# A chunked linear recurrence and a mixture of experts: decays and y kept in the buffer that w is loaded into, and a new order of steps

## The chip, the cores and the metric

The kernel runs on one core of one Trainium2 chip. The metric is the device time of one execution in microseconds (us). The engines are TensorE (PE for its matmuls, PEld for its weight loads), VectorE (DVE), ScalarE (ACT), GpSimd (POOL) and SyncE (SP, which here only issues transfers). Each engine takes its instructions strictly in the order in which the program gives them to it, and waits on semaphores where an instruction needs another engine's result.

## The reference

Two parts follow one another. The first is a recurrence over 768 steps, for 4 batches of 8 heads, each with a 40 x 40 state:

```python
for t in range(S):                       # r, k, v, w, a, b: (4, 8, 768, 40)
    y[:, :, t] = einsum('bhd,bhde->bhe', r_t, state)
    Sa = einsum('bhde,bhe->bhd', state, a_t)
    state = state * w_t[:, :, None, :] - einsum('bhd,bhe->bhde', Sa, b_t)
    state = state + einsum('bhd,bhe->bhde', v_t, k_t)
```

The second takes y as 3072 rows of 320 and sends each row to one of 8 experts: logits = x @ w_gate, the largest logit names the expert and its softmax is the weight, at most 768 rows go to an expert, in order of the rows; each expert computes relu(x @ w1) @ w2 with a hidden width of 1024, and the weight scales its row of the output.

## The kernel before

**Tiling.** The 768 steps are cut into six blocks i of 128, and a block into two chunks c of 64. The four batches make two pairs, pr = 0 and 1; a pair's two batches lie on partitions 0 to 39 and 64 to 103 of a buffer, each half of 64 partitions, so instructions that span both work on 104 partitions and rows 40 to 63 must hold zeros (or values that meet zeros).

**Stages of one block.** `prep` loads `w`, `a`, `kb` and `rv` and makes the decays on DVE: `scan_g` (L315) a scan from right to left into `gx`, `scan_p` (L325) one from left to right into `px`; `mul_a` (L331) and `mul_kb` (L336) multiply them into `a` and `kb`. `unit` makes three products per chunk: `nn`, which ACT copies into `ns`; `kk`, which DVE masks into `tm` (L381); and `iden`, which ACT copies into `bk`. `inverse` inverts the triangular matrices of both pairs and both chunks together on DVE: a transpose `begin2` (L485), 31 pairs of rows (L432 a product into `tmp`, L433 a sum into `nu`), called the elimination here, and two transposes back, `back_a` (L437) and `back_b` (L441); `comb` (L453, L469) puts the 32-wide parts together on PE and ACT to `nt`. `chain` then walks the chunks: from the state (`D` for pair 0, `E` for pair 1) over `zs`, `vu` and `snew` to the next state (DVE L596, L599), and aside from that `qp` (a mask on DVE, L640) and y. `take_y` (L667) scales y by `px` into `yE`. `gate` transposes y (L711), makes the logits (L716), and stores the rows; `route` places them with indirect transfers. When all six blocks are routed, a count of the fullest expert is cast to an integer (`maxc`, L1229), on whose value a branch hangs, and the experts follow with weights streamed from memory.

**What sets the order.** The code of a stage doesn't run where it is written: `steps(name)` collects threads of steps, each with the engine it uses and a planner's time for it, what it needs and gives, and which buffers it takes and frees. `Schedule.order` plays these threads against each other with those times and emits the steps in the order that results; a table `later` can move a thread, and `mu` and `tail` weigh the due time and the length of what follows. A step can't be placed before its buffers are free. `BUFS` says how many there are of each: three of `px`, two each of `w` and `yE`. A `px` is taken in `scan_p` and freed by the second chunk's `take_y`:

```python
add(scan_p, "V2.8", take=["px"], free=["w"], gives=("px", n))
...
more(take_y, "V.69", take=["yE"] * (1 - c), free=["pp"] + ["px"] * c, gives=("y", n))
```

**Start.** DVE clears PSUM, `w` and a helper `z2`; POOL clears rows 32 to 63 and 96 to 127 of `a`, `kb` and `rv` (L262), then other buffers, `gx`'s last column (L266) among the later ones.

## Time and profile before

| | |
|---|---|
| median of 3 runs (lowest to highest) | 921.32 us (919.52 to 922.74) |
| the profiled execution: time, and its span | 922.49 us, 920.8 us |
| busy: PE, DVE, ACT, POOL | 611.3, 463.2, 212.5, 155.7 us |
| mean granted TensorE clock, as a share of the full one | 0.782 |
| recurrence with routing; experts | to 639; from 639 to 921 us |

The span runs from the first to the last instruction of the profiled execution. An engine's busy time is a sum over stages that have different limits. The TensorE clock has two levels, 1.2 GHz (0.50) and 2.4 GHz (1.00); a value between them is a mean over a stretch.

### The profile page before, as it was taken

The numbers are of one execution on the slowest core, as the hardware profiler recorded it, in microseconds if no ns is written. First come the engines' busy times: TensorE is split into PE (matmuls) and PEld (weight loads), VectorE is DVE, ScalarE is ACT, GpSimd is POOL, SyncE is SP. The second block draws the span as 40 slices with busy tenths as digits, with TensorE's granted clock in tenths as the row PEclk, the third lists the DMA queues.
The fourth block names the chain that finished last, engine by engine and source line by source line (L and its number), as shares of the span: only waits on it lengthen the run. The fifth ranks groups of instructions, "written<-read, shape, count | busy, mean of one in ns | idle before, by whom it ended". The sixth has DMA issues, their size and how long they took to land. (4 is left out here: it accounts for less than half of the span.)

```text
span 920.8 us, 30344 instructions
## 1 busy us (share of the span) xinstructions
PE 611.3 (66%) x13828; PEld 483.9 (53%) x13828; DVE 463.2 (50%) x853; ACT 212.5 (23%) x444; POOL 155.7 (17%) x203
## 2 busy tenths in 40 slices
PE   0306776197836877198736886385079999988893
PEld 0305666196736766197636776385026665445542
DVE  5794339923686256923587347733423334432320
ACT  0002322022112222032111222121324333442230
POOL 9700000001000010001000100011333233223321
PEclk9957997569655897558765797577579999999987
DMA  3401133022401143012320212001985855576410
GB/s 97 140 22 48 40 88 83 1 73 69 89 15 57 40 74 103 1 38 75 53 84 1 49 37 59 18 4 47 243 133 145 198 129 148 155 203 154 126 50 17
DMA packets 77662, 73.83 MB, mean 80 GB/s; under 512 B 46857, under 2 KB 69387, under 8 KB 75604
## 3 DMA queue, kind: packets, MB, share of 16 engines
q1 hardware_dynamic: 68116, 54.50, 24.3%
q0 software_dynamic: 4224, 9.89, 3.7%
q10 hardware_dynamic: 5184, 7.41, 2.9%
q8 instruction: 110, 1.80, 0.9%
q14 instruction: 28, 0.23, 0.1%
HBM read 56.77 MB, written 10.08 MB: 73 GB/s over the span
## 5 line engine op out<-in xcount | busy, mean ns | idle before, releaser
L1142 PE MATMUL ps<-xT,w 128*128 128x480 f16 (+1 forms) x512 | 112.7, 387 | 49.2 <-DMA mm<-meta 36.4
L977 DVE SCALAR_TENSOR_TENSOR w<-s,w 128x640 f16<-128x640 f32 (+1 forms) x56 | 54.0, 994 | 110.0 <-ACT w L976 109.7
L1142 PEld LDWEIGHTS <-w 128*128 128x128 f16 (+1 forms) x512 | 46.6, 101 | 114.8 <-issue 78.3
L1037 PE MATMUL ps<-w,hh 128*128 128x320 f16 (+1 forms) x768 | 106.1, 299 | 0.0
L1037 PEld LDWEIGHTS <-hh 128*128 128x128 f16 (+1 forms) x768 | 79.0, 104 | 26.4 <-issue 1.1
L252 PE MATMUL p<-a,kb 64*64 64x64 f32 x768 | 43.2, 294 | 62.6 <-DVE a L331 58.1
L976 ACT ACTIVATE w<-s 128x640 f16<-128x640 f32 (+1 forms) x56 | 46.6, 871 | 116.6 <-DMA s<-in_moe_w_dram 111.9
L453 PE MATMUL p<-nu,ns 32*32 32x32 f32 x768 | 22.3, 233 | 77.1 <-DVE nu L441 42.0
L252 PEld LDWEIGHTS p<-a,kb 64*64 64x64 f32 x768 | 39.3, 202 | 64.4 <-DVE a L331 58.4
L433 DVE TENSOR_TENSOR nu<-nu,tmp 128x31 f32<-128x31 f32 (+15 forms) x186 | 63.8, 343 | 6.4
L432 DVE TENSOR_TENSOR tmp<-xu,nu 128x31 f32<-128x31 f32 (+15 forms) x186 | 63.6, 342 | 6.5
L1152 DVE SCALAR_TENSOR_TENSOR hh<-ps,hh 128x480 f16<-128x480 f32 x64 | 39.0, 651 | 53.1 <-ACT hh L1149 53.0
L453 PEld LDWEIGHTS p<-nu,ns 32*32 32x32 f32 x768 | 20.7, 148 | 78.4 <-DVE nu L441 42.5
L424 POOL MEMSET nu<- 128x1024 f32 x6 | 5.7, 953 | 328.1 <-PE p L453 328.1
L1041 POOL DMA_INDIRECT out_dram<-ob,ri x32 | 34.8, 1088 | 149.9 <-ACT ob L1168 76.1
L252 PE MATMUL pp<-a,kb 64*32 64x64 f32 (+1 forms) x1536 | 32.0, 257 | 39.9 <-DVE z L314 36.8
L902 POOL DMA_INDIRECT meta<-mt,sloti x24 | 23.7, 986 | 186.6 <-DVE mt L899 146.3
L252 PEld LDWEIGHTS pp<-a,kb 64*32 64x32 f32 x1536 | 28.7, 138 | 42.8 <-issue 34.9
L640 DVE TENSOR_TENSOR qp<-pp,mask 128x1024 f32<-128x1024 f32 x24 | 29.1, 1221 | 27.0 <-PE pp L252 26.8
L252 PE MATMUL pp<-ident,kb 64*64 64x40 f32 x1536 | 33.6, 241 | 12.8 <-issue 9.3
L381 DVE TENSOR_TENSOR tm<-p,mask 128x512 f32<-128x512 f32 x24 | 16.3, 681 | 51.3 <-PE p L252 51.1
L1149 ACT ACTIVATE hh<-ps 128x480 f16<-128x480 f32 x64 | 32.9, 566 | 35.2 <-PE ps L1142 35.1
(141 smaller groups left out, 1024.3 us busy)
## 6 DMA issues: line engine op xcount, KB each, us to landing
s<-in_moe_w_dram SPq DMA_DIRECT2D x16, 512.0 KB
kb<-in_kb_dram SPq DMA_DIRECT2D x24, 320.0 KB
rv<-in_rv_dram SPq DMA_DIRECT2D x24, 320.0 KB
s<-in_moe_w_dram ACTq DMA_DIRECT2D x17, 320.0 KB
...
```

The lines of the kernel that those rows point to most:

```text
L252: TT.matmul(out, l, r, start=start, stop=True, skip_group_check=True)
L432: V.tensor_mul(tv, xu[:, s + 1:, s:s + 1].to_broadcast([P, n, m]), nu[:, s:s + 1, 0:m].to_broadcast([P, n, m]))
L433: V.tensor_add(nu[:, s + 1:, 0:m], nu[:, s + 1:, 0:m], tv)
L453: TT.matmul(p[C * z + 32:C * z + 64, u * 32:u * 32 + 32], G_["ns"][lo, pr * 16 + u, 32:C], s_["n1"][lo, pr * 16 + u, :], start=True, stop= ...
L640: V.tensor_mul(U["qp"].rearrange("p r u t -> p (r u) t"), U["pm"].rearrange("p r (u t) -> p (r u) t", t=C), mk(16))
L976: return (lambda: nc.scalar.activation(h, s(), AF.Copy, scale=SW), lambda: nc.vector.scalar_tensor_tensor(l, s(), SW, h, ALU.mult, ALU.sub ...
L977: lambda: nc.vector.scalar_tensor_tensor(l, s(), SW, h, ALU.mult, ALU.subtract))
L1037: nc.tensor.matmul(po[:, :DM], h[l], rr[:, f, :], start=(f == 0 and m == 0), stop=(f == NF - 1 and m == 2))
L1041: nc.gpsimd.indirect_dma_start(out=out[:, :], out_offset=bass.IndirectOffsetOnAxis(ap=ri.bitcast(U32)[:c, j, 1:2], axis=0), in_=ob[:c], in ...
L1142: nc.tensor.matmul(s_["h", f + z][:, :n], l, rr, start=m % 7 == 0 and m < 14, stop=m >= 14)
L1149: nc.scalar.activation(s_["hh"][:, 0, f, :n], s_["h", f][:, :n], AF.Relu)
L1152: nc.vector.scalar_tensor_tensor(s_["hh"][:, 1, f, :n], s_["h", f][:, :n], 0.0, s_["hh"][:, 0, f, :n], ALU.max, ALU.subtract)
```

## The change

`w` is loaded into `px` itself, one column to the right, by one transfer of 128 partitions (the host packs a third group of rows so that all 128 are defined) in place of two of 40; column 0 is cleared by DVE in `scan_g`. `scan_p` and `take_y` write where they read, so that `px` holds w, then the decay, then the scaled y, and is freed after the logits; `w` and `yE` go. There are six `px`, and one more of `a`, `tm` and `nt`. Zero rows of `a`, `kb` and `rv` come by 16 transfers from a cleared tile of 24 rows. The logits are made in quarters: for each head, each half of the partitions (a batch) and each half of the columns (a chunk) a matmul of its own. The planner's times for some steps, its latencies and weights are other numbers, and `later` has a table; of those numbers a few lines stand here. A choice between ACT and DVE for a copy goes to DVE only where it would end 1.05 us earlier by the planner.

```diff
@@ -156,7 +156,7 @@
                         ends.append(z + d[-1] + 0.9)
                         end = max(end, ends[-1])
                     else:
-                        end = max(end, s0 + hold + 0.12)
+                        end = max(end, s0 + hold + (0.34 if e == "P" else 0.14))
...
-    MU = 0.004
-    O_TAIL = 0.004
+    MU = 0.0036902
+    O_TAIL = 0.0016952
...
-    BUFS = {"pp": 3, "p1": 2, "w": 2, "gx": 1, "px": 3, "a": 3, "kb": 2, "rv": 2, "tm": 4, "ns": 1, "xu": 1, "nu": 1,
-            "nt": 3, "qq": 1, "bk": 5, "vu": 4, "zs": 2, "uE": 2, "qp": 2, "Sd": 3, "yE": 2, "x16": 2, "D": 2, "E": 2,
+    BUFS = {"pp": 3, "p1": 2, "gx": 1, "px": 6, "a": 4, "kb": 2, "rv": 2, "tm": 5, "ns": 1, "xu": 1, "nu": 1,
+            "nt": 4, "qq": 1, "bk": 5, "vu": 4, "zs": 2, "uE": 2, "qp": 2, "Sd": 3, "x16": 2, "D": 2, "E": 2,
             "g0": 4}
...
-    sch = Schedule(nc, free_, MU, O_TAIL, O_BIAS, (0.8, 0.0, 0.0), {})
+    LATER = {"chain": -0.01, "comb": -0.66, "decay": 0.12, "decay_k": 0.2, "fill": 36.07, "gate": -0.24,
+             "iden": -0.05, "inverse": 0.1, "inverse_": -46.42, "kk": -0.36, "load_a": 1.12, "load_kb": -1.45,
+             "load_rv": 7.56, "load_v": 5.54, "load_w": -2.65, "lower": 0.24, "nn": -1.22, "out": -0.04,
+             "route": 0.03, "saT": -18.52, "turn": 0.48, "unit": -16.96, "zz": 0.22}
+    sch = Schedule(nc, free_, MU, O_TAIL, O_BIAS, (1.05,) * 3, LATER)
...
-    for n, x in enumerate(free_["pp"] + free_["p1"]):
+    zero = one.tile([24, 2 * H * P], F32, name="zero")
+    V.memset(zero, 0.0)
+    z2 = one.tile([P, H, P + 1], F32, name="z2")
+    V.memset(z2, 0.0)
+    for x in free_["a"] + free_["kb"] + free_["rv"]:
+        n = x.rearrange(("p h t -> p (h t)", "p z h t -> p (z h t)", "p z c u t -> p (z c u t)")[len(x.shape) - 3])
+        for lo in (D, C + D):
+            nc.sync.dma_start(n[lo:lo + 24], zero[:, 0:n.shape[1]])
+    for x in free_["pp"] + free_["p1"]:
         V.memset(x, 0.0)
-    for n, x in enumerate(free_["w"]):
-        (V, G)[n % 2].memset(x, 1.0)
-        (V, G)[n % 2].memset(x[:, :, 0:1], 0.0)
-    for n, x in enumerate(free_["a"] + free_["kb"] + free_["rv"]):
-        for lo in (32, 96):
-            G.memset(x[lo:lo + 32], 0.0)
     for x in free_["zs"] + free_["D"] + free_["E"]:
```

```diff
+        def load_w():
+            T["px"] = get("px")
+            dma(T["px"][:, :, 1:], w[pr, i].rearrange("e (h t) -> e h t", h=H))
+
+        steps("load_w")(load_w, "L0>2.7", take=["px"], gives=("load_w", n))
...
             if i:
                 T["g0"] = get("g0")
             V.memset(z2[0:R, :, 0:1], 1.0)
+            V.memset(T["px"][:, :, 0:1], 0.0)
             V.tensor_tensor_scan(T["gx"][0:R, 0:H * (P + 1)][:, ::-1],
-                                 T["w"][0:R].rearrange("p h t -> p (h t)")[:, ::-1],
+                                 T["px"][0:R].rearrange("p h t -> p (h t)")[:, ::-1],
                                  z2[0:R].rearrange("p h t -> p (h t)")[:, ::-1], 1.0, ALU.mult, ALU.add)
 
         def scan_p():
-            T["px"] = get("px")
             g3 = T["gx"][0:R, 0:H * (P + 1)].rearrange("p (h t) -> p h t", t=P + 1)
             if i:
                 V.tensor_copy(T["g0"][0:R, :], g3[:, :, 1])
             V.reciprocal(z2[0:R, :, 0], g3[:, :, 1])
             V.tensor_tensor_scan(T["px"][0:R].rearrange("p h t -> p (h t)"),
-                                 T["w"][0:R].rearrange("p h t -> p (h t)"),
+                                 T["px"][0:R].rearrange("p h t -> p (h t)"),
                                  z2[0:R].rearrange("p h t -> p (h t)"), 1.0, ALU.mult, ALU.add)
-            put("w", T["w"])
...
         add = steps(f"decay{pr}")
-        add(scan_g, "V2.5", take=["gx"] + ["g0"] * (i > 0), needs=[("load_w", n)])
-        add(scan_p, "V2.8", take=["px"], free=["w"], gives=("px", n))
+        add(scan_g, "V2.7", take=["gx"] + ["g0"] * (i > 0), needs=[("load_w", n)])
+        add(scan_p, "V2.8", gives=("px", n))
...
         def take_y():
-            if c == 0:
-                T["yE"] = get("yE")
             p = U["py"]
-            V.scalar_tensor_tensor(T["yE"][0:R, :, ct].rearrange("p (r k) t -> p r k t", r=2),
+            V.scalar_tensor_tensor(T["px"][0:R, :, ct].rearrange("p (r k) t -> p r k t", r=2),
                                    p[0:R, :, 0:256].rearrange("p r (k t) -> p r k t", k=4), SX,
                                    T["px"][0:R, :, ct].rearrange("p (r k) t -> p r k t", r=2), ALU.mult, ALU.mult)
             put("pp", p)
-            if c:
-                put("px", T["px"])
...
@@ -695,9 +697,9 @@
         more(mT_v, "P.65", needs=[("load_rv", (pr, i)), ("uE", n)], take=["pp"])
         more(mT_u, "P.65", needs=[("uE", n)], free=["uE"])
         more(take_m, "V1.22", take=["qp"], free=["pp"])
-        more(yy, "P1.6", needs=[("bk", n)] + [("Sd", n)] * (q > 0), take=["pp"],
+        more(yy, "P1.6", needs=[("bk", n)] + [("Sd", n)] * (q > 0) + [("snew", n)] * (q < NQ - 1), take=["pp"],
              free=["qp", "bk", "vu"] + ["Sd"] * (q > 0) + ["rv"] * c)
-        more(take_y, "V.69", take=["yE"] * (1 - c), free=["pp"] + ["px"] * c, gives=("y", n))
+        more(take_y, "V.69", free=["pp"], gives=("y", n))
...
     def gate(T):
@@ -708,13 +710,15 @@
         def turn_y():
             p = Q["pt"] = get("pp")
             for h in range(H):
-                TT.transpose(p[:, h // 4, h % 4 * P:h % 4 * P + R], T["yE"][0:R, h, :], ident[0:R, 0:R])
+                TT.transpose(p[:, h // 4, h % 4 * P:h % 4 * P + R], T["px"][0:R, h, 0:P], ident[0:R, 0:R])
 
         def logits():
             p = Q["pt"]
             for h in range(H):
-                TT.matmul(p[:, 0, R:R + 16], T["yE"][0:R, h, :], wge[0:R, h, :], start=h == 0, stop=h == H - 1)
-            put("yE", T["yE"])
+                for x in range(2):
+                    for c in range(2):
+                        mm(p[half(c), x, R:R + 8], T["px"][half(x), h, half(c)], wge[half(x), h, :], h == 0)
+            put("px", T["px"])
...
         def take_logits():
             t = pr * NI + i
-            scale(lg[:, t::2 * NI, :], Q["pt"][:, 0, R:R + 16].rearrange("p (x e) -> p x e", x=2), 1.0 / SX)
...
-    wge = glob.tile([104, H, 2 * E], F32, name="wge")
+    wge = glob.tile([P, H, E], F32, name="wge")
     nc.gpsimd.memset(wge, 0.0)
     for x in range(2):
-        nc.sync.dma_start(wge[64 * x:64 * x + D, :, x * E:x * E + E], w_gate.rearrange("(h d) e -> d h e", d=D))
+        nc.sync.dma_start(wge[64 * x:64 * x + D], w_gate.rearrange("(h d) e -> d h e", d=D))
...
     out = {x: inputs[x] for x in ("moe_w_gate", "moe_w1", "moe_w2", "moe_capacity")}
-    out["w"] = rows(inputs["w"])
+    x = rows(inputs["w"])
+    out["w"] = np.concatenate([x, x[:, :, :, 0:C - D]], 3).reshape(B // 2, NI, P, H * P)
```

How the order moves, in three places. Rows are an engine's instructions in their order: source line, operation, what is written <- what is read, with buffer numbers, and the shape. First DVE, ahead of and into the elimination of block 2 (the third), before; L667 is the last y of block 1, pair 1, L325 the second decay of block 2, L485 `begin2`:

```order
L596 TENSOR_TENSOR E_153<-p_1_103,g_3_157 104x8x40
L667 SCALAR_TENSOR_TENSOR yE_147<-pp_101,px_107 104x8x64
L323 COPY g_0_154<-gx_106 104x8
L324 RECIPROCAL z_188<-gx_106 104x8
L325 SCALAR_TENSOR_TENSOR px_107<-w_104,z_188 104x1032
L336 TENSOR_TENSOR kb_113<-kb_113,gx_106 104x2048
L485 STREAM_TRANSPOSE xu_122<-ns_121 128x1024
L432 TENSOR_TENSOR tmp<-xu_122,nu_123 128x31
L433 TENSOR_TENSOR nu_123<-nu_123,tmp 128x31
```

and in the changed kernel, eleven rows in the elimination of block 2, from its seventh row on (L438 and L439 are the former L432 and L433, L605 the new state of block 1, L387 a masked `tm`, L646 a `qp`):

```order
L438 TENSOR_TENSOR tmp<-xu_125,nu_126 128x112
L439 TENSOR_TENSOR nu_126<-nu_126,tmp 128x28x4
L605 TENSOR_TENSOR D_152<-p_0_102,D_153 104x8x40
L438 TENSOR_TENSOR tmp<-xu_125,nu_126 128x135
L439 TENSOR_TENSOR nu_126<-nu_126,tmp 128x27x5
L387 TENSOR_TENSOR tm_120<-p_1_103,mask 128x512
L646 TENSOR_TENSOR qp_145<-pp_99,mask 128x1024
L438 TENSOR_TENSOR tmp<-xu_125,nu_126 128x156
L439 TENSOR_TENSOR nu_126<-nu_126,tmp 128x26x6
L438 TENSOR_TENSOR tmp<-xu_125,nu_126 128x175
L439 TENSOR_TENSOR nu_126<-nu_126,tmp 128x25x7
```

The elimination stood in one piece behind the last y of the block before; now its pairs of rows stand between the steps of the chain of block 1, from the first new state on (in blocks 1 to 5 alike, 62 rows in groups of 2 to 10).

Second SP's queue, the first transfers before:

```order
L828 DMA wge<-in_moe_w_gate_dram 40x8x8 x2
L62 DMA w_104<-in_w_dram 40x8x128 x2
L62 DMA kb_113<-in_kb_dram 40x2048 x2
L62 DMA a_110<-in_a_dram 40x1024 x2
L62 DMA w_105<-in_w_dram 40x8x128 x2
L62 DMA vu_133<-in_vt_dram 64x320 x2
L62 DMA rv_115<-in_rv_dram 40x2048 x2
```

and now (`zero` is the cleared tile, a_111 to rv_118 the buffers that get zero rows):

```order
L62 DMA px_105<-in_w_dram 128x8x128
L832 DMA wge<-in_moe_w_gate_dram 40x8x8 x2
L266 DMA a_111<-zero 24x1024 x2
L266 DMA a_112<-zero 24x1024 x2
L266 DMA a_113<-zero 24x1024 x2
L266 DMA a_114<-zero 24x1024 x2
L266 DMA kb_115<-zero 24x2048 x2
L266 DMA kb_116<-zero 24x2048 x2
L266 DMA rv_117<-zero 24x2048 x2
L266 DMA rv_118<-zero 24x2048 x2
L62 DMA kb_115<-in_kb_dram 40x2048 x2
L62 DMA px_106<-in_w_dram 128x8x128
```

The first `w` went from behind `wge` to the front, and 16 transfers of zeros stand between it and the first `kb`.

Third PE, at the gate of block 0, pair 0, before (yE_146 holds y, pp_101 is PSUM):

```order
L252 MATMUL pp_99<-D_151,a_112 64x40 x16
L610 MATMUL p_0_102<-ident,D_151 128x104 x4
L711 MATMUL pp_101<-ident,yE_146 128x104 x8
L252 MATMUL pp_99<-vu_135,tm_118 64x40 x16
L716 MATMUL pp_101<-wge,yE_146 128x16 x8
L252 MATMUL p_0_102<-a_110,kb_114 64x64 x32
```

and now, for both pairs (px_105 and px_106 hold y):

```order
L713 MATMUL pp_100<-ident,px_105 128x104 x8
L256 MATMUL pp_100<-wge,px_105 64x8 x32
L256 MATMUL pp_99<-vu_137,tm_123 64x40 x16
L713 MATMUL pp_101<-ident,px_106 128x104 x8
L256 MATMUL pp_99<-D_153,a_113 64x40 x16
L256 MATMUL pp_101<-wge,px_106 64x8 x32
```

The gates of block 0 stand ahead of the `comb` of block 1 now, and a row of 8 matmuls with 128 columns of weights became one of 32 with 64.

## Rows read from the trace of the kernel before

**Rows 1.** The page: the span; busy us, share and instructions of each engine.

```profile
span 920.8 us, 30344 instructions
...
PE 611.3 (66%) x13828; PEld 483.9 (53%) x13828; DVE 463.2 (50%) x853; ACT 212.5 (23%) x444; POOL 155.7 (17%) x203
```

**Rows 2.** Timeline of DVE: start us, us; first and sixth back_b, and the cast.

```profile
74.84 1.25 DVE L441 STREAM_TRANSPOSE nu<-xu 128x1024 f32<-128x1024 f32 x1
...
589.12 1.25 DVE L441 STREAM_TRANSPOSE nu<-xu 128x1024 f32<-128x1024 f32 x1
...
639.09 0.11 DVE L1229 CAST maxc<-m 1x1 int32<-1x1 f32 x1
```

**Rows 3.** Windows of the two stages of one block.

```profile
core 0: us, PE busy (x) PEld busy (x) DVE busy (x) ACT busy (x) POOL busy (x), PEclk, DMA share, GB/s
181.60:254.10 72.50, 61.27 (x1942) 55.76 (x1942) 31.23 (x54) 16.51 (x42) 6.49 (x7) 0.74 0.31 76
254.10:287.00 32.90, 10.39 (x197) 9.83 (x199) 30.61 (x71) 3.75 (x10) 0.00 (x0) 0.53 0.02 6
```

**Rows 4.** Waits of PE, 74 to 590 us: total us, times, longest us.

```profile
PE p L252 <- DVE a L331: 58.1, 3, 19.8
PE pp L252 <- issue: 43.2, 41, 3.8
...
PE p L453 <- DVE nu L441: 20.1, 2, 18.6
PE pp L252 <- ACT bk L402: 5.3, 5, 1.1
PE pp L252 <- ACT vu L47: 5.1, 10, 1.0
...
PE pp L252 <- ACT ns L51: 2.5, 4, 0.8
PE pp L711 <- ACT zs L47: 1.7, 3, 0.6
...
PE p L252 <- issue: 1.5, 4, 0.6
PE pp L252 <- ACT zs L47: 0.6, 1, 0.6
```

**Rows 5.** Timeline of DVE ahead of the third elimination.

```profile
239.66 0.07 DVE L314 MEMSET z<- 104x8 f32 x1
...
248.10 0.68 DVE L667 SCALAR_TENSOR_TENSOR yE<-pp,px 104x512 f32<-104x512 f32 x1
...
249.01 2.31 DVE L325 TENSOR_TENSOR_SCAN px<-w,z 104x1032 f32<-104x1032 f32 x1
251.23 2.27 DVE L336 TENSOR_TENSOR kb<-kb,gx 104x2048 f32<-104x2048 f32 x1
254.16 1.94 DVE L485 STREAM_TRANSPOSE xu<-ns 128x1024 f32<-128x1024 f32 x1 [0.66 <-ACT ns L51]
```

**Rows 6.** Groups by line, 74 to 590 us: busy us, mean ns.

```profile
L433 DVE TENSOR_TENSOR nu<-nu,tmp 128x31 f32<-128x31 f32 (+15 forms) x155 | 53.2, 343 | 5.3
...
L252 PE MATMUL pp<-ident,kb 64*64 64x40 f32 x1536 | 33.6, 241 | 12.8 <-issue 9.3 <-ACT ns L51 2.3 <-ACT bk L402 1.1
...
L716 PE MATMUL pp<-wge,yE 104*128 104x16 f32 x160 | 29.4, 331 | 0.0
```

**Rows 7.** Windows of one block, and behind the last elimination; columns as above.

```profile
185.00:200.00 15.00, 15.00 (x422) 14.40 (x409) 2.06 (x9) 4.12 (x10) 2.22 (x2) 0.50 0.29 87
205.00:220.00 15.00, 11.61 (x512) 10.05 (x505) 5.41 (x7) 3.39 (x8) 0.00 (x0) 1.00 0.28 79
240.00:250.00 10.00, 9.14 (x128) 8.46 (x130) 4.94 (x7) 0.83 (x3) 0.00 (x0) 0.50 0.57 145
262.00:280.00 18.00, 1.85 (x9) 1.74 (x9) 16.59 (x43) 0.83 (x3) 0.00 (x0) 0.50 0.00 0
...
590.00:602.00 12.00, 10.90 (x252) 10.53 (x254) 3.97 (x21) 3.66 (x9) 1.94 (x2) 0.50 0.11 36
```

**Rows 8.** Timelines of DVE and of POOL at the start.

```profile
11.35 2.31 DVE L315 TENSOR_TENSOR_SCAN gx<-w,z 104x1032 f32<-104x1032 f32 x1 [2.33 <-DMA w<-in_w_dram]
...
13.93 2.31 DVE L325 TENSOR_TENSOR_SCAN px<-w,z 104x1032 f32<-104x1032 f32 x1
27.71 2.29 DVE L336 TENSOR_TENSOR kb<-kb,gx 104x2048 f32<-104x2048 f32 x1 [11.47 <-POOL mlo L274]
...
9.99 7.36 POOL L262 MEMSET kb<- 32x2048 f32 x4
17.40 7.35 POOL L262 MEMSET rv<- 32x2048 f32 x4
...
27.58 0.10 POOL L266 MEMSET gx<- 128x1 f32 x1
```

**Rows 9.** Timeline of SP's issues, and windows with DMA share and GB/s.

```profile
14.00 0.70 SPq L62 DMA_DIRECT2D a<-in_a_dram  x2
...
12.00:18.00 6.00, 0.00 (x0) 0.00 (x0) 4.17 (x3) 0.00 (x0) 5.84 (x4) 1.00 0.53 136
18.00:24.00 6.00, 0.00 (x0) 0.00 (x0) 0.00 (x0) 0.00 (x0) 5.84 (x4) 1.00 0.72 216
24.00:30.00 6.00, 0.00 (x0) 0.00 (x0) 2.29 (x2) 0.00 (x0) 5.52 (x17) 1.00 0.70 220
```

**Rows 10.** Waits of DVE, 74 to 590 us.

```profile
DVE tm L381 <- PE p L252: 51.1, 13, 7.3
DVE yE L667 <- PE pp L252: 31.3, 15, 3.3
...
DVE D L599 <- PE p L252: 22.9, 4, 7.5
DVE qp L640 <- PE pp L252: 21.4, 13, 4.6
DVE D L596 <- PE p L252: 17.2, 5, 5.0
DVE E L599 <- PE p L252: 9.8, 4, 3.0
```

More of the change, by code (lines that the diff above doesn't have):

```diff
@@ L107, in order @@
         for x in reversed(ready):
-            own = sum(max((2.2 + d[-1] if len(d) > 1 else d[0] + 0.12) for _, d in par) for par in threads[x[0]][x[1]][1][0])
+            own = sum(max((2.2 + d[-1] if len(d) > 1 else d[0] + 0.2) for _, d in par) for par in threads[x[0]][x[1]][1][0])
             tail[x] = own + max([tail[y] for y in after[x]] or [0.0])
@@ L237, in scan_part @@
              "vu": ([P, 2, H, D], F32), "zs": ([P, H, C], F32), "uE": ([P, H, C], F32), "qp": ([P, 2, H, C], F32),
-             "Sd": ([P, 2, 4, D], F32), "yE": ([P, H, P], F32), "x16": ([P, 2, 2, 384], F16),
+             "Sd": ([P, 2, 4, D], F32), "x16": ([P, 2, 2, 384], F16),
              "D": ([P, 4, 2, C], F32), "E": ([P, 4, 2, C], F32), "g0": ([P, H], F32)}
@@ L266, in scan_part @@
         G.memset(x[:, H * (P + 1):], 1.0)
-    z2 = one.tile([P, H, P + 1], F32, name="z2")
-    V.memset(z2, 0.0)
     mask = one.tile([P, C], F32, name="mask")
@@ L290, in prep, with loads @@
         n = (pr, i)
-        def loads(name, kind, src, rows, cols=lambda y: y):
+        def loads(kind, src, rows):
             def go():
@@ L295, in go @@
                 for z in range(2):
-                    dma(rows(T[kind])[half(z, D)], cols(src[pr, i, z]))
+                    dma(rows(T[kind])[half(z, D)], src[pr, i, z])
             return go
-        add = steps("load_w")
-        add(loads("w", "w", w, lambda x: x[:, :, 1:], lambda y: y.rearrange("e (h t) -> e h t", h=H)), "L0>.86&L0>.86", take=["w"], gives=("load_w", n))
-        steps("load_a")(loads("a", "a", a, lambda x: x.rearrange("p h t -> p (h t)")), "L0>.86&L0>.86", take=["a"],
+        def load_w():
+            T["px"] = get("px")
+            dma(T["px"][:, :, 1:], w[pr, i].rearrange("e (h t) -> e h t", h=H))
+        steps("load_w")(load_w, "L0>2.7", take=["px"], gives=("load_w", n))
+        steps("load_a")(loads("a", a, lambda x: x.rearrange("p h t -> p (h t)")), "L0>.86&L0>.86", take=["a"],
                         gives=("load_a", n))
-        steps("load_kb")(loads("kb", "kb", kb, lambda x: x.rearrange("p z h t -> p (z h t)")), "L0>1.7&L0>1.7",
+        steps("load_kb")(loads("kb", kb, lambda x: x.rearrange("p z h t -> p (z h t)")), "L0>1.7&L0>1.7",
                          take=["kb"], gives=("load_kb", n))
         PLAN[0] += HC / 2
-        steps("load_rv")(loads("rv", "rv", rv, lambda x: x.rearrange("p z c u t -> p (z c u t)")), "L0>1.7&L0>1.7",
+        steps("load_rv")(loads("rv", rv, lambda x: x.rearrange("p z c u t -> p (z c u t)")), "L0>1.7&L0>1.7",
                          take=["rv"], gives=("load_rv", n))
@@ L488, in inverse @@
         add = steps("inverse")
-        add(begin2, "V1.22", needs=[("nn", (pr, 2 * i + c)) for pr in range(2) for c in range(2)] + [("unit", i)], take=["xu"])
+        add(begin2, "V1.97", needs=[("nn", (pr, 2 * i + c)) for pr in range(2) for c in range(2)] + [("unit", i)], take=["xu"])
         for s in range(31):
             add(lambda s=s: elim(s), f"V{((31 - s) * (s + 1) + 150) / 960 * 2:.3f}")
-        add(back_a, "V1.22", gives=("ntd", i))
+        add(back_a, "V1.94", gives=("ntd", i))
         add(back_b, "V1.22", gives=("n1", i))
@@ L498, in inverse @@
             add(lambda pr=pr: take_a(pr), "A.62|V.69", take=["qq"], free=["p1"] + ["ns", "nu"] * pr)
-            add(lambda pr=pr: comb_b(pr), "P1.7", take=["p1"], free=["qq"])
+            add(lambda pr=pr: comb_b(pr), "P2.6", take=["p1"], free=["qq"])
             add(lambda pr=pr: take_b(pr), "A.62|V.69", needs=[("lower", pr, i)], free=["p1"] + ["xu"] * pr,
@@ L685, in chain @@
         if q < NQ - 1:
-            add(snew, "P.9" if c else "P.6", needs=[("bk", n)], take=["p1"])
+            add(snew, "P.9" if c else "P.6", needs=[("bk", n)], take=["p1"], gives=("snew", n))
             add(take_snew, "V.49", needs=([("turned", n)] if q else []) + ([("px", (pr, i + 1))] if c else []),
@@ L739, in take_logits @@
             t = pr * NI + i
-            scale(lg[:, t::2 * NI, :], Q["pt"][:, 0, R:R + 16].rearrange("p (x e) -> p x e", x=2), 1.0 / SX)
+            scale(lg[:, t::2 * NI, :], Q["pt"][:, :, R:R + 8], 1.0 / SX)
         def store_x():
@@ L749, in gate @@
         add(turn_y, "P1.0", needs=[("y", (pr, 2 * i)), ("y", (pr, 2 * i + 1))], take=["pp"])
-        add(logits, "P1.0", free=["yE"])
+        add(logits, "P.6", free=["px"])
         add(take_logits, "A.2|V.2", gives=("logits", n))
```

2 lines of the change are left out of this document (1 added, 1 removed).

## The prediction

> **What bounds the kernel now.** I read the page's busy table first [rows 1]: of a span of 920.8 us PE is busy 66% and DVE 50%, so no engine is full. The times of one instruction that comes once per block, the second transpose behind the elimination (`back_b`), show the beat [rows 2]: the first starts at 74.84, the sixth at 589.12, so the five blocks between them take (589.12 - 74.84) / 5 = 102.9 us each. Ahead of them lie 75 us of start, behind them 332 us: 50 us until `maxc` is cast at 639.09, then the experts.
>
> Inside one block (180.4 to 284.8, taken as 181.6 to 287.0) the windows show two stages that take turns [rows 3]. For 72.5 us PE is the busy one (61.3 us) and DVE works 31.2 us; for 32.9 us DVE works 30.6 us and PE 10.4 us. The second stage is the elimination: it is solid on DVE, and PE ends it waiting, 58.1 us in 3 waits and 20.1 us in 2 in this part of the run [rows 4]. Nothing in the mathematics asks for turns: the elimination of block i+1 doesn't use the chain of block i. The timeline shows what does [rows 5]: the last scaled y of a pair (L667) at 248.10 is followed at once by the scan that writes `px` (L325, 249.01), then `kb`, then at 254.16 the transpose that opens the elimination. The order names the buffer: L667 reads px_107, L325 overwrites px_107. With three `px`, the next block's second decay can't be made before this block's last y, so its elimination starts when the chain is over.
>
> **The change part by part.**
>
> *Six `px` and the new order.* px_107 is no longer waited for: three pairs of buffers hold the decays of the chain's block, of the next, and a load. In the new order the elimination's pairs of rows (L438, L439) stand between the chain's own DVE steps, and so do the second scan and a multiply. What this is worth is a new length of the beat, which I bound from DVE and from PE.
>
> DVE: its busy time in a block is 31.23 + 30.61 = 61.8 us [rows 3], and the change takes almost nothing from it (the two copies `vu` and `zs` that DVE made now and then go to ACT, which is busy 20.3 us of 105). So the beat can't be under 62 us.
>
> PE: 61.27 + 10.39 = 71.7 us busy [rows 3]. To it come stalls in which PE waits for nothing that the profile shows, 43.2 + 1.5 over five blocks, 8.9 us each, and waits for ACT's copies, (5.3 + 5.1 + 2.5 + 1.7 + 0.6) / 5 = 3.0 us [rows 4]; both stay with PE wherever DVE's elimination lies. That makes 83.6 us. Two things are taken off.
> - Logits: now 29.4 us for 160 instructions, ten gates, 2.9 us each, 5.9 us in a block [rows 6]. They become 64 instructions of 64x64 by 8 per gate. No row shows that form; the nearest is the 64x64 by 40 against the identity, 33.6 us for 1536, so 64 of them 1.4 us [rows 6]. Moving 8 columns in place of 40 may be cheaper, and four quarters in the array of which each writes its own place may be no faster than one; between 0.7 and 2.9 us per gate I take the row, 1.4: 3.0 us less in a block, 80.6 us.
> - Clock: after the elimination PE runs at 0.50, the lower of its two levels (1.2 GHz): 422 matmuls in 15.0 busy us, 36 ns each, against 512 in 11.6 us, 23 ns each, at 1.00 later in the block [rows 7]. Behind a PE idle for most of 18 us comes this slow stretch; without the idle time I expect most of it to go. It and the other slow stretch shown (9.1 us) are 24.1 us; at 23/36 of the time they would be 15.4, so 8.7 us less. Of this I take 8, since the gaps don't all go: 72.6 us.
>
> To it I add 1.4 us for turns: twelve chain steps on DVE (four new states, four masks, four y) now stand behind a pair of rows, a row 0.34 us in the mean [rows 6], so each is late by up to 0.7 us, and I choose that PE has other work in hand for five in six of them (12 x 0.7 / 6 = 1.4). Beat: 74 us, PE-bound. The chain's step now waited for in DVE's queue is the new state (L605): behind it stand pairs of the elimination, for which comb of the next block waits on PE. That is why the two sums are not independent and why the 62 us will not be reached.
>
> Bounds of the beat: below, all of PE's slow time gone (the second stage's 10.4 us at 0.53 [rows 3] too, together 34.5 us, worth 12.4 in place of 8) and half the stalls hidden in waits: 74 - 4.4 - 4.5 - 1.4 = 63.7, just over DVE's 62. Above, no better clock and no better logits: 83.6. Five beats: 5 x (102.9 - 74) = 144.5 us less, between 96.5 and 196.
>
> *Zero rows by transfers.* DVE's first `kb` multiply waits 11.47 us, until POOL has filled `kb`, `rv` and `gx` at 27.6 [rows 8]. POOL loses the fills of `a`, `kb`, `rv` and `w`; the zeros come over SP's queue, ahead of the first `kb` load. That is 16 transfers in 8 rows of the order, 4 x 2 x 24 rows of 4 KB and 8 x 24 of 8 KB, 2.36 MB in all. Issue: a pair without backlog took 0.70 us, so 16 take 5.6 us [rows 9]. Moving: at the 216 to 220 GB/s that loads reached here [rows 9] 10.8 us. They start when DVE has set `zero`, near 3 us; so they end near 14, `kb` (0.66 MB) 3 us later, and with a microsecond to land the multiply starts near 18 in place of 27.71: 9.7 us less. DVE's row order behind it is nearly that of before. The price has an end on either side: at the 136 GB/s of 12 to 18 us [rows 9] they take 17.4 us, and the gain is 3; if they hide, the multiply starts when the scans end, at 16.24 now and with `w` there in time 2.33 us earlier [rows 8]: 13.9, a gain of 13.8. The Trainium skill ("DMA: Bandwidth & Descriptors", section "Why a DMA increments its semaphore by 16 and not by 1") says that a transfer runs on the largest number of engines up to 16 that divides its rows, so 24 rows get 12 and loads of 40 rows 10. The trace agrees roughly for the loads: the DMA share is 0.70 to 0.72, not near 1, with loads of 40 rows and some of 64 in flight. By it the zeros would move 12/10 as fast, an estimate of 9 us in place of 10.8, and the gain would be 11.
>
> *Decay in place, y in place, `w` as one transfer of 128 rows.* The scans keep form and length; each gains a memset of column 0 (0.07 us, as L314 in [rows 5]), 0.14 us in a block. `w` moves 524 KB in place of 328 per load, 2 loads a block, over a DMA that is 31% and 2% busy [rows 3]; hidden, and if not, 2 us a block at 216 GB/s.
>
> *The end.* From 590 to 602 PE runs at 0.50 behind the last elimination [rows 7]. With PE busy ahead of it, 10.9 us shrink by a third: 4 us less. The experts are unchanged.
>
> **Sum** against the profiled execution, 922.49 us (1.69 around its span; 0.13% over the median of 921.32): 922.5 - 144.5 - 9.7 - 4.0 = 764 us.
>
> **The rivals.**
> 1. *Turns cost more.* The chain comes late by what the eliminations take, and DVE still waits for PE at the chain's steps. For it speaks that DVE now waits (31.3 + 22.9 + 21.4 + 17.2 + 9.8) / 5 = 20.5 us per block there and 51.1 / 5 = 10.2 at `tm` [rows 10]; if all that stays on top of 61.8, the beat is 92.5 us and the time 922.5 - 52 - 13.7 = 857. Against it: while it waits, DVE now has rows of the elimination to do. Part of it (a beat from 85 on) is likelier than all of it: 820 to 857.
> 2. *PE at half clock throughout (slower).* Place: the chain stage, now at 0.74 in the mean [rows 3]. With a pair of rows between any two turns PE has short gaps all over; if it never leaves 0.50, the 71.7 - 24.1 = 47.6 us that aren't at 0.50 in the two stretches shown take 36/23 as long, 74.5, and the beat is 74.5 + 24.1 + 8.9 + 3.0 - 3.0 = 107.5: 922.5 + 23 - 9.7 = 936 us. It decides from a beat of 102.9 + 9.7/5 = 104.8 us on. Against it: from 205 to 220 PE is busy 77% with such gaps, and has 1.00 [rows 7]. The Trainium skill ("TensorE: Matmul & The Clock Gate", "A second HAM failure mode: psum-queue depth-cycling") tells of a kernel whose small gaps between groups of matmuls made the clock swing; the trace has the swing behind the elimination, but not in 205 to 220.
> 3. *The change doesn't do what it says:* some other buffer (`rv`, `kb`, `pp`) takes the place of `px`, the beat stays within 3 us of 102.9 and only start and end gain: 894 to 924. Against it: the order itself has the eliminations between the chain's steps, and in-order engines can't put them back.
>
> **How the numbers follow.** Main case 709 (922.5 - 196 - 13.8 - 4) to 820 (922.5 - 96.5 - 3 - 3 for an end half as warm): chance 0.81, 764 its likeliest. Below it 0.01. Rival 1: 0.12. Rival 3: 0.03, of it 0.01 without change. Rival 2: 0.03. The range is the main case, 709 to 820; what lies outside it is 0.19. A measurement of this kernel tells 0.3% from no change; by the same cases it is faster by more with 0.96, within it with 0.01, slower by more with 0.03.
>
> **What would show it.** Right: `back_b` starts 74 us apart (64 to 84), DVE busy over 75% in a block, no PE wait of 18 us for L441 or L331's like, clock over 0.85 from block to block, first `kb` multiply near 18 us, 64 logit instructions in some 1.4 us. Wrong: a clock near 0.5 in the blocks (rival 2), DVE waits of 20 us or more per block at L605, L646, L671 (rival 1), or PE stalls that grow with its density beyond 9 us a block.

## The result and the profile after

The changed kernel took 796.5 us (median of 4 runs, 791.24 to 798.89) against 922.03 for the kernel before: a ratio of 0.863, 95% interval 0.857 to 0.868. Six more of its runs, on another chip, gave 0.862 (0.858 to 0.866). The prediction was 764, its range 709 to 820. The profiled execution took 798.89 us.

The page of the changed kernel, span and busy table, to be held against [rows 1]: PE is busy 73% in place of 66%, and for 30.5 us less.

```profile
span 796.9 us, 31433 instructions
...
PE 580.8 (73%) x14404; PEld 456.1 (57%) x14404; DVE 446.5 (56%) x845; ACT 218.3 (27%) x467; POOL 133.2 (17%) x183
```

The answers to [rows 2] are in the timeline of DVE of the changed kernel:

```profile
76.66 1.25 DVE L447 STREAM_TRANSPOSE nu<-xu 128x1024 f32<-128x1024 f32 x1
...
452.30 1.25 DVE L447 STREAM_TRANSPOSE nu<-xu 128x1024 f32<-128x1024 f32 x1
...
501.54 0.11 DVE L1233 CAST maxc<-m 1x1 int32<-1x1 f32 x1
```

These marks (the start of the span, the first and the last `back_b`, the cast, the end of the span) cut it into four stages, and the whole difference is placed. The five beats take (452.30 - 76.66) / 5 = 75.1 us each in the mean in place of 102.9: 138.6 us less, where 144.5 were forecast. Single beats take 66.4, 80.2, 73.9, 81.6 and 73.6 us, so 75.1 is a mean of unlike ones. The start is 1.8 us longer (76.66 to 74.84), where 9.7 less were forecast. From the last `back_b` to the cast it is 49.2 to 50.0: 0.7 less, forecast 4. And from the cast to the end it is 295.4 in place of 281.7: 13.6 us more, where the prediction had "The experts are unchanged". Of the spans, 920.8 - 138.6 + 1.8 - 0.7 + 13.6 is 796.9.

Inside the beats, first the window of the five beats of the kernel before, and of its waits of PE there one that [rows 4] doesn't show:

```profile
74.90:589.20 514.30, 342.90 (x11008) 311.72 (x11008) 295.83 (x580) 104.62 (x253) 28.48 (x35) 0.72 0.21 53
```

```profile
PE p L453 <- DVE tm L381: 35.1, 3, 30.9
```

Then the window of the changed kernel, and the waits of PE and of DVE in it:

```profile
76.70:452.30 375.60, 302.59 (x11008) 275.37 (x11008) 279.41 (x568) 103.01 (x259) 28.87 (x32) 0.81 0.25 67
```

```profile
PE pp L256 <- issue: 46.1, 44, 3.9
PE p L459 <- DVE nu L447: 11.7, 3, 9.9
PE p L459 <- ACT nt L51: 4.3, 2, 2.2
PE p L256 <- issue: 3.5, 4, 1.4
PE p L475 <- ACT qq L47: 3.5, 4, 1.5
PE p L459 <- issue: 3.5, 2, 2.9
PE p L928 <- issue: 3.4, 1, 3.4
...
DVE tm L387 <- PE p L256: 25.0, 11, 4.3
DVE qp L646 <- PE pp L256: 20.7, 11, 6.0
DVE px L671 <- PE pp L256: 17.2, 14, 4.5
DVE tm L387 <- PE pp L256: 9.4, 4, 4.1
DVE E L605 <- PE p L256: 3.7, 3, 2.9
```

PE is busy 302.59 / 5 = 60.5 us per beat; of its 73.0 idle us in the window, 56.5 are stalls in which it waits for nothing that the profile shows. PE's waits of 58.1 us ([rows 4]) and 35.1 us for DVE are gone, the second of which the prediction hadn't listed; of the 20.1 us behind `back_b` [rows 4] 11.7 are left, of which 9.9 stand behind the first `back_b`. DVE is busy 279.41 / 5 = 55.9 us, 74% of the beat, and still waits at `tm`, the mask and `y`. The clock is 0.81 where it was 0.72 before.

### The profile page after: what moved, and what is told of

Read it like the earlier page. It is cut to its first block, busy times and chain, and to the rows that moved or that the text cites. A ratio compares the mean times of both kernels' runs of the same rounds, so it can differ in the third digit from the quotient of the medians.

```text
span 796.9 us, 31433 instructions
## 1 busy us (share of the span) xinstructions
PE 580.8 (73%) x14404; PEld 456.1 (57%) x14404; DVE 446.5 (56%) x845; ACT 218.3 (27%) x467; POOL 133.2 (17%) x183
## 5 line engine op out<-in xcount | busy, mean ns | idle before, releaser
L1146 PE MATMUL ps<-xT,w 128*128 128x480 f16 (+1 forms) x512 | 106.7, 373 | 37.0 <-DMA mm<-meta 37.0
L1041 PE MATMUL ps<-w,hh 128*128 128x320 f16 (+1 forms) x768 | 114.5, 311 | 23.9 <-ACT hh L1153 21.9
L439 DVE TENSOR_TENSOR nu<-nu,tmp 128x31 f32<-128x31 f32 (+15 forms) x186 | 63.9, 344 | 6.4
L438 DVE TENSOR_TENSOR tmp<-xu,nu 128x31 f32<-128x31 f32 (+15 forms) x186 | 62.9, 338 | 3.8
L256 PE MATMUL pp<-a,kb 64*32 64x32 f32 (+1 forms) x1536 | 32.2, 261 | 37.8 <-DVE px L322 31.3
L646 DVE TENSOR_TENSOR qp<-pp,mask 128x1024 f32<-128x1024 f32 x24 | 29.2, 1222 | 28.3 <-PE pp L256 28.3
L475 PE MATMUL p<-xu,qq 32*64 32x32 f32 x768 | 41.6, 281 | 4.2 <-ACT qq L47 4.2
L475 PEld LDWEIGHTS p<-xu,qq 32*64 32x64 f32 x768 | 40.0, 210 | 5.4 <-ACT qq L47 4.8
L1172 ACT ACTIVATE ob<-ps,gs 128x320 f32<-128x320 f32 (+1 forms) x32 | 16.8, 526 | 84.3 <-PE ps L1041 68.9
L256 PE MATMUL p<-a,kb 64*64 64x64 f32 x768 | 38.5, 271 | 1.4 <-issue 1.4
L1019 POOL DMA_INDIRECT xt<-xd,ri x32 | 37.9, 1183 | 8.7 <-issue 7.0
L256 PE MATMUL pp<-ident,kb 64*64 64x40 f32 x1536 | 30.6, 229 | 9.5 <-issue 9.3
```

The source lines that it names most:

```text
L256: TT.matmul(out, l, r, start=start, stop=True, skip_group_check=True)
L438: V.tensor_mul(tv, xu[:, s + 1:, s:s + 1].to_broadcast([P, n, m]), nu[:, s:s + 1, 0:m].to_broadcast([P, n, m]))
L439: V.tensor_add(nu[:, s + 1:, 0:m], nu[:, s + 1:, 0:m], tv)
L475: TT.matmul(p[half(z), u * 32:u * 32 + 32], s_["qq"][hi, u, :], s_["ntd"][hi, pr * 16 + u, :], start=True, stop=True)
L1019: nc.gpsimd.indirect_dma_start(out=xt[:c, j].rearrange("p a c -> p (a c)"), out_offset=None, in_=xd[:, :], in_offset=bass.IndirectOffsetOn ...
L1041: nc.tensor.matmul(po[:, :DM], h[l], rr[:, f, :], start=(f == 0 and m == 0), stop=(f == NF - 1 and m == 2))
```

## The experiments

Each ratio is to the kernel before on the same chip. There it took 921.9 us for the first four kernels below, 938.5 for the two with old or new numbers and the two with more work, and 924.8 for the kernel without LATER, the one with four `px` and the last two.

**Experts planned by the old waits.** The constants 0.34 and 0.14 stand in a class that plans the experts too.

```
-    def __init__(self, nc, bufs, mu, tail, bias, alt=(100.0,) * 3, later={}):
+    def __init__(self, nc, bufs, mu, tail, bias, alt=(100.0,) * 3, later={}, lat=(0.12, 0.12)):
...
+        self.lat = lat
...
-                        end = max(end, s0 + hold + (0.34 if e == "P" else 0.14))
+                        end = max(end, s0 + hold + (self.lat[0] if e == "P" else self.lat[1]))
...
-    sch = Schedule(nc, free_, MU, O_TAIL, O_BIAS, (1.05,) * 3, LATER)
+    sch = Schedule(nc, free_, MU, O_TAIL, O_BIAS, (1.05,) * 3, LATER, (0.34, 0.14))
```

> The changed kernel, with the order of the experts planned by the old waits between engines (0.12 for all) and that of the scan by the new ones (0.34 behind PE, 0.14 elsewhere); PE's order is the same in both. Theory A: the experts lost 13.6 us (cast of maxc to the end 281.7 before, 295.4 after) because their own order was set anew by the shared constants, which shows as ACT's hh late for PE (21.9 us of waits). Then cast to end goes back to 280 to 285 us, the waits on ACT's hh fall under 5 us, and the time is 783 to 787. Rival B: the loss comes from what the scan leaves behind (DMA traffic, the clock, the state of the queues at the hand-over); then cast to end stays at 293 to 297 and the time at 795 to 800.

786.98 us (785.33 to 789.4; ratio 0.852, 0.847 to 0.857); cast to end 287.4, between the two forecasts. Waits of PE in that stage, first of the changed kernel, then of this one:

```profile
...
PE ps L1041 <- ACT hh L1153: 21.9, 5, 9.9
PE ps L1041 <- DVE hh L1156: 2.0, 6, 0.5
```

```profile
...
PE ps L1147 <- DMA xT<-xt: 12.9, 4, 4.5
PE ps L1042 <- DVE hh L1157: 3.0, 3, 1.5
PE ps L1042 <- ACT hh L1154: 0.5, 1, 0.5
```

The longest of these waits in the changed kernel, in the timelines of ACT and PE (`w` is a cast of weights, `s` their load):

```profile
589.75 0.74 ACT L980 ACTIVATE w<-s 128x640 f16<-128x640 f32 x1 [13.34 <-DMA s<-in_moe_w_dram]
590.39 1.01 ACT L1153 ACTIVATE hh<-ps 128x480 f16<-128x480 f32 x2
...
591.00 0.71 PE L1041 MATMUL ps<-w,hh 128*128 128x320 f16 x2 [9.90 <-ACT hh L1153]
```

In the new order the `hh` that PE needs next stands in ACT's queue behind a cast of weights that waits for its load. PE's four long waits (9.90, 6.11, 4.00 and 1.74 us, 21.75 of the 21.9) come behind waits of ACT for that load of 13.34, 9.54, 7.43 and 5.17 us. In the old order PE waits 0.5 us for ACT's `hh`, and 12.9 for `xT`, as before (12.8). Over all profiles, nine with the new order of the experts took 290.1 to 298.4 us from cast to end, 293.3 in the mean; those with the old order took 281.8, 282.3, 284.9 and 287.4, and before 281.7, 283.6 in the mean. So A has the cause, for some 10 of the 13.6 us; the rest is within the spread of this stage.

**Zeros behind the loads.**

```
-    for x in free_["a"] + free_["kb"] + free_["rv"]:
...
-            nc.sync.dma_start(n[lo:lo + 24], zero[:, 0:n.shape[1]])
+    new = {id(x) for y in ("a", "kb", "rv") for x in free_[y]}
...
                     dma(rows(T[kind])[half(z, D)], src[pr, i, z])
+                if id(T[kind]) in new:
+                    new.discard(id(T[kind]))
+                    n = rows(T[kind])
+                    for lo in (D, C + D):
+                        nc.sync.dma_start(n[lo:lo + 24], zero[:, 0:n.shape[1]])
```

> The changed kernel, with the 16 transfers of zeros not ahead of all loads but two by two behind the first load of the buffer that they belong to; nothing else moves. Theory A: the start gained nothing since 16 issues (14.6 us) and 2.36 MB stand ahead of the first kb load. Then the first kb multiply starts at 14.5 to 18 us in place of 26.51, the first back_b at 64 to 70 in place of 76.66, and the time falls by 7 to 12 us. Rival B: the start is bound by bytes whichever comes first (loads of 3.0 MB and zeros of 1.2 MB before the second pair's multiplies, 28 us at 150 GB/s); then the first multiply is early but the second pair's stays near 36 to 38, back_b comes at 73 to 77 and the time falls by 0 to 3 us.

784.85 us (780.85 to 788.0; ratio 0.850, 0.844 to 0.855). Timelines of SP's issues and of DVE in the changed kernel:

```profile
3.07 6.23 SPq L266 DMA_DIRECT2D a<-zero  x8
9.35 3.28 SPq L266 DMA_DIRECT2D kb<-zero  x4
12.67 5.12 SPq L266 DMA_DIRECT2D rv<-zero  x4
17.84 2.54 SPq L62 DMA_DIRECT2D kb<-in_kb_dram  x2
...
26.51 2.29 DVE L342 TENSOR_TENSOR kb<-kb,gx 104x2048 f32<-104x2048 f32 x1 [11.62 <-DMA kb<-in_kb_dram]
```

and in this kernel:

```profile
2.61 1.03 SPq L62 DMA_DIRECT2D kb<-in_kb_dram  x2
3.69 1.69 SPq L302 DMA_DIRECT2D kb<-zero  x2
...
14.82 2.26 DVE L344 TENSOR_TENSOR kb<-kb,gx 104x2048 f32<-104x2048 f32 x1
...
27.51 1.22 DVE L339 TENSOR_TENSOR a<-a,px 104x1024 f32<-104x1024 f32 x1 [3.76 <-DMA a<-zero]
```

The multiply starts as soon as the scan ends, the first `back_b` at 65.88: 10.8 us earlier. A holds in full. The zeros had cost SP 14.6 us of issue (6.23 + 3.28 + 5.12), and the `kb` load stood behind all of them.

**Zeros by POOL in the order of need.** `kb` and the first two `a` are filled by POOL first (memsets of 32 rows, with `gx`'s last column ahead of them), the other `a` last, `rv` by transfers behind its load.

> The changed kernel, with the zero rows of kb and a filled by POOL in the order in which they are needed, and those of rv by transfers behind the first load of rv. By POOL's rows of the kernel before (1.84 us for half a kb, 0.97 for half an a) kb and a of the first block are ready at 15. Theory A (the transfers cost the start): first kb multiply when the second scan ends, 14.5 to 17; back_b at 62 to 67 in place of 76.66; time lower by 9 to 14 us. Rival B (the start is bound by the loads themselves): back_b stays at 73 to 77, time lower by 0 to 3 us. If both this and the kernel with transfers behind the loads gain alike, it was the place in the queue and not the engine that makes the zeros.

779.62 us (775.49 to 782.63; ratio 0.844, 0.838 to 0.849); first multiply 15.80, first `back_b` 66.75, 9.9 us earlier. The time fell by 16.9, more than A allows; of the rest 5.2 are the experts (290.2 in this profile). Both mends gain the same at the start, so it was the place in the queue, not the engine that makes the zeros.

**Logits as before.** The layout of `wge` and the copy of the logits go back with them.

```
-    for x in range(2):
-        for c in range(2):
-            mm(p[half(c), x, R:R + 8], T["px"][half(x), h, half(c)], wge[half(x), h, :], h == 0)
+    TT.matmul(p[:, 0, R:R + 16], T["px"][0:R, h, 0:P], wge[0:R, h, :], start=h == 0, stop=h == H - 1)
```

> The changed kernel, with the logits of a gate as 8 matmuls of 104 rows and 16 columns on 128 lines of y again, in place of 64 quarters of 8 columns; the order is the same. Theory A: the beat is bound by PE, so 2.9 us per gate in place of 1.23 is 3.3 us per block and some 20 us over 12 gates: 812 to 820. Rival B: PE waits for DVE often enough, at half of the places, that a longer logit goes into slack: 0 to 8 us more. A third, C: the old form isn't slower here (2.9 us was at half clock); then the logits take under 1.6 us and the time is that of the changed kernel.

796.41 us (median of six, 782.65 to 815.47, a wide spread), 0.864 of the kernel before; the two shortest alone give 0.853 (0.846 to 0.860), so whether this kernel is as fast as the changed one or 1% faster is open. Its beat is 74.9. None of the three forecasts came in the form it had. Groups by line of the changed kernel, then of this one:

```profile
L256 PE MATMUL pp<-wge,px 64*64 64x8 f32 x640 | 12.3, 205 | 1.1 <-issue 1.1
```

```profile
L718 PE MATMUL pp<-wge,px 104*128 104x16 f32 x154 | 20.1, 272 | 0.0
```

The five beats of this kernel and its largest entry of stalls, to be held against 302.59 and 46.1:

```profile
76.90:451.40 374.50, 313.87 (x10522) 286.53 (x10522) 279.56 (x569) 103.64 (x259) 29.07 (x32) 0.79 0.24 67
```

```profile
PE pp L256 <- issue: 36.8, 36, 3.3
```

The trace holds two records for each of the program's matmuls here: 16 per gate in the old form, 64 in quarters, so there are four times as many, and not 64 for 8 as the expectation has it. The old form takes 20.1 / 154 x 16 = 2.1 us per gate to 1.23, and PE is busy 11.3 us more in the five beats, of which the logits are 7.8. But all stalls without a cause together are 45.5 us, where six profiles of this order with quarters have 51.2 to 59.9 (the changed kernel 56.5). So PE's busy time and stalls add up to the same, and the 3.0 us per block that the prediction took off for quarters aren't there. That the quarters make these stalls is argued and not shown: at their own rows stand only 1.1 us.

**Old numbers in the changed kernel; new numbers in the kernel before.** The first puts MU, O_TAIL, 0.12, the old costs, the old choice between ACT and DVE and an empty LATER into the changed kernel, the second the new ones into before, which keeps its buffers and its experts' order.

> All of the changed kernel (six px, decay and y in place, zeros by transfers, logits in quarters) with the numbers that set the order as they were: MU, O_TAIL, waits of 0.12, the old costs of begin2, back_a and comb_b, no LATER. Theory A: the buffers carry the beat, since any order can then put the next elimination into the chain; beat 74 to 80 us, time 785 to 820 (the experts' order too is the old one). Rival B: the numbers carry it; with the old ones, which favour long tails, the next blocks' eliminations and scans run ahead as a solid piece and PE waits for them; beat 85 to 100, time 840 to 920.

> The kernel before (three px, w in buffers of its own, memsets by POOL, old logits) with the new numbers alone. Theory A: without the buffers the second decay of the next block can't be made before this block's last y, whatever the numbers say; beat 98 to 108, time 905 to 950. Rival B: the numbers alone give a good part; beat under 92, time under 870.

885.16 us (ratio 0.944, 0.938 to 0.950), beat 89.7: rival B, and only its first two beats (68.8, 71.4) are short, then come 106.1, 104.8 and 97.2. And 905.99 us (ratio 0.967, 0.960 to 0.973), beat 97.3: theory A, nearly. All but the numbers (the buffers, and with them zeros, quarters and the rest) saves 13.2 us of a beat, numbers alone 5.6 (15 and 7 if the 1.8% by which that chip is slower are taken off), together 27.7. With old numbers PE stands before `comb` and the chain again; waits of PE in the five beats of the changed kernel with the old numbers:

```profile
PE p L459 <- DVE E L607: 28.0, 1, 28.0
PE p L256 <- DVE E L605: 17.2, 1, 17.2
```

**No LATER.** All else new.

> The changed kernel with the table LATER empty; all other numbers new. With all numbers old the beat was 89.7. Theory A: the longer waits and the costs carry the order (a step that ends on PE is planned 0.34 later, so chain steps are put further apart and rows of the elimination fill them); beat 75 to 79, time 795 to 820. Rival B: the table carries it; beat 82 to 92, time 835 to 900.

873.31 us (865.61 to 879.21; ratio 0.943, 0.937 to 0.949), beat 86.8: B. The table that shifts each kind of step in the planner's choice carries 12 us of each beat (the changed kernel had 74.8 on that chip), and PE's waits show the same place (`comb` behind a DVE that is at something else):

```profile
PE p L459 <- DVE tm L387: 28.5, 2, 27.7
```

**Four `px`.** `"px": 6` becomes `"px": 4`.

> The changed kernel with four buffers of px in place of six; the numbers that set the order are the same. Theory A: the chain's block and the next one hold two pairs, and the third pair is needed as the one into which w is loaded ahead: with four, w of block i+2 can't be loaded until y of block i has gone through the gate, the second decays come late and the beat is 82 to 100, time 830 to 920. Rival B: two pairs are enough, since a load of 524 KB takes about 3 us and there is room for it; beat 75 to 78, time 795 to 812.

872.68 us (865.24 to 875.77; ratio 0.944, 0.939 to 0.949), beat 84.4: A. Waits of DVE between the first and the last `back_b`, where the changed kernel has 17.2:

```profile
DVE px L671 <- PE pp L256: 83.1, 14, 16.0
```

For the load of `w` itself DVE waits only 2.8 us: it stands at y, in its own order. The numbers were the same, so they may fit six better than four; that a third pair is needed under any numbers isn't shown.

**More work for DVE, more for PE.** In the first, `if s % 2: V.tensor_mul(tv, ...)` repeats the product before it is added; in the second, `for h in 3 * list(range(H))` repeats the quarters of the logits.

> The changed kernel, with 15 of the 31 products of each elimination made twice (the second over the first), 5.6 us more of DVE per block by 0.36 us a row; the order is the same else. Theory A: PE bounds the beat (60.5 us busy, 11.3 of stalls, 3 of waits for others), so DVE's 19 idle us take most of it up: beat 75 to 77, time up by 3 to 15 us. Rival B: neither engine bounds it alone, the turns between them do, so what DVE does longer stands in the chain's way: beat 78 to 81, time up by 20 to 38 us.

> The changed kernel, with each gate's 64 quarters made three times over (each time from a fresh start), 128 instructions and 2.5 us of PE more per gate, 5 us in a block; the old form instead of quarters cost PE 2.25 us more in a block and had 1.9 us less of stalls, so 256 more instructions may bring 4.3 us of stalls as well. Theory A: PE bounds the beat; it grows by 5 to 9 us, time up by 30 to 55 us. Rival B: PE has slack at the gates; beat up by 0 to 2, time up by 0 to 12 us. In between, the slack at the gates is finite and its size is what is left over.

820.45 us (ratio 0.875, 0.870 to 0.881) and 849.15 (0.907, 0.901 to 0.913), where the changed kernel has 0.863: 12 and 42 us more of that chip's 938.5. The beats are 78.1 and 83.6, of which the slower chip may be 1.4 (1.8% of 75). The first has the time of A and, with 1.4 taken off, its beat; the second is A. DVE's busy time grew by 4.8 us a beat (303.6 / 5 to 55.9) and cost 1.6 to 3.0. Groups by line of the kernel with the logits made three times, and its five beats:

```profile
L256 PE MATMUL pp<-wge,px 64*64 64x8 f32 x1792 | 34.4, 210 | 9.1 <-issue 9.0
```

```profile
77.00:494.80 417.80, 346.44 (x12160) 313.72 (x12160) 280.66 (x569) 103.06 (x260) 28.77 (x32) 0.76 0.22 60
```

34.4 + 9.1 in place of 12.3 + 1.1 for ten gates: 3.0 us per gate, 6.0 in a block, a quarter of it stalls. The beat grew by more, 7.0 to 8.4: PE is busy 346.4 / 5 = 69.3 us, 8.8 more, of which the logits are 4.4, and the granted clock was 0.76 for 0.81. PE with its stalls bounds the beat in the main; DVE's 19.2 idle us (75.1 - 55.9) take up between a third and two thirds of what it is given, not all.

**The changed kernel again, and both mends.** The second has the zeros by POOL and the experts by the old waits.

> The changed kernel once more, with nothing edited, as the measure for the three others of this group. Theory: 0.857 to 0.868 of the kernel before; beat 74.5 to 75.5; from the cast of maxc to the end 290 to 296 us, since the four kernels measured that share the experts' order of the changed kernel took 290.1 to 293.6. If it lies under 288, the experts' loss is chance and not order.

> The changed kernel, with zeros of kb and a by POOL in the order of need and those of rv behind rv's first load, and with the experts' order planned by the old waits. Theory A: both gains add, since they lie in stages that don't overlap: back_b first at 66 to 67, beat 74.5, 50 us to the cast, 282 to 287 after it: 773 to 779 us, 18 to 23 less than the changed kernel on the same chip. Rival B: an earlier start is given back at the hand-over to the experts (the weights' loads come no earlier); then 780 to 786.

795.2 us (792.46 to 804.59), beat 74.8, cast to end 290.6. And 777.64 us median of six runs from 762.56 to 782.68; since one of them lies apart from the rest, no interval of the ratio is given. It is 17.6 us under the changed kernel on the same chip. In the profiles (791.7 and 778.0) the first `back_b` is 11.3 us earlier and the experts 5.7 shorter, while the five beats are 5.0 longer (75.8 each): the gains of both stages are there, and A's time, though not the equal beat.

## Why the prediction was right, point by point

- **Six `px` and the new order**: the mechanism holds. The elimination lies inside the chain, and PE's long waits for it went. What the prediction treated as one cause is two that need each other: of 27.7 us a beat, 13.2 come without the numbers and 5.6 with the numbers alone.
- **The beat, 75.1 for 74**: PE's busy time came out at 60.5 for the sum's 71.7 - 3.0 - 8 = 60.7, and that is luck, with a base and a saving that are both too large. The base of 71.7 us is one block's; the mean of five was 342.9 / 5 = 68.6. And these five hold 480 matmul records of preparation that the five beats of the changed kernel don't: it makes nearly all of them ahead of its first `back_b`, where PE is busy for 19.7 us in place of 9.0. By the means of the kernel before they are 13.4 us, or 2.7 a beat. From the 65.9 that are left it fell by 5.4. Of this the logits are 5.9 - 2.5 = 3.4; by the run with the old form, 2 x (2.1 - 1.23) = 1.7 of them are the form (3.0 forecast), and the rest is the clock that the gates ran at (3.5 us per gate at 0.50 and 2.0 at 1.00 before). For the clock and whatever else changed that leaves some 3.7, where 8 were forecast. Stalls are 11.3 for 8.9, over the 9 that was named as a sign of being wrong; with the logits of before all stalls were 2.2 a block less, so the quarters, if it is they that make the difference, are worth about nothing. PE's other idle time is (73.0 - 56.5) / 5 = 3.3 us for 3.0 + 1.4. DVE's floor of 62 us was too high too: it was busy 295.8 / 5 = 59.2 us a beat before and is 55.9 now.
- **Clock: the slow stretch did not go.** The prediction put it down to a PE idle for 18 us. Around the third `back_b` of the changed kernel the windows show it behind an idle time of 3.4 us only; the last row is from the end (columns as in [rows 3]):

```profile
203.00:208.00 5.00, 1.64 (x56) 1.33 (x57) 1.74 (x5) 0.00 (x1) 0.00 (x0) 0.93 0.28 43
208.00:213.00 5.00, 4.50 (x112) 4.13 (x111) 2.08 (x4) 0.00 (x0) 0.00 (x0) 0.50 0.02 3
213.00:223.00 10.00, 10.00 (x256) 8.89 (x252) 6.75 (x15) 2.93 (x12) 0.00 (x0) 0.60 0.30 95
223.00:233.00 10.00, 7.81 (x226) 7.45 (x226) 9.83 (x12) 3.79 (x10) 0.00 (x0) 0.57 0.51 157
233.00:243.00 10.00, 10.00 (x278) 9.55 (x274) 7.29 (x16) 2.76 (x5) 2.26 (x3) 0.50 0.35 107
243.00:253.00 10.00, 8.87 (x405) 8.39 (x403) 6.49 (x16) 2.60 (x7) 0.00 (x0) 0.91 0.01 3
...
460.00:470.00 10.00, 10.00 (x287) 9.68 (x285) 1.80 (x9) 2.62 (x6) 2.97 (x4) 0.50 0.42 111
```

  From 208 to 243 it is at 0.50 to 0.60, at the lower level (1.2 GHz) most of the time, with PE busy 32.3 of 35 us; the stretch that [rows 7] shows a part of ran from 182 to 202. This is the longest: at 148 to 166, 298 to 316 and 382 to 400 the clock is at 0.50 to 0.54 for 18 us. "Over 0.85 from block to block" was wrong: 0.81. What sets it here stays open; no run changed it alone.
- **Zero rows by transfers, +1.8 in place of -9.7**: the term failed in both its parts. 16 issues took 14.6 us, not 5.6, at 0.8 to 1.3 us each, one behind the other, so the `kb` load was issued at 17.84; and from there it took 8.7 us to the multiply (26.51), where 3 and 1 were forecast. The zeros moved at 131 to 164 GB/s, between the 136 of the far end and the 216 of the main case: the bound left out that issue and move hold up the load one behind the other. So the first multiply came 1.2 us earlier (26.51 for 27.71) and not 9.7, and with 2.7 us of waits for `a` behind it, of which there were none before, the first `back_b` came 1.8 later. Two kernels show the gain of some 10 us where the zeros don't stand ahead of the load.
- **The end, -0.7 in place of -4**: in the last row above PE is busy all the time at 0.50; the stretch behind the last elimination is as slow as before, so a third of 10.9 us was never to be had.
- **"The experts are unchanged"** is the step that failed by most, 13.6 us. The diff's two constants in `walk` stand in the class that orders the experts as well; the prediction read them for the scan alone. That the time still lies in the range is owed to the beats, whose bounds lie some 50 us to either side; start and experts came out beyond what their terms allowed.
- **Rivals.** DVE's waits at the chain's steps are there, as rival 1 had them, but they shrank to 8.7 us a beat (20.5 before) and those at `tm` to 6.9 (10.2); DVE now does elimination in between. Rival 2's low clock stands in the stretches above, not throughout. Of rival 3 nothing is seen.
